# One more zero matmul per unit in twelve stretches of a four-layer attention kernel

## The chip, the core and the metric

The kernel runs on one core of one Trainium2 chip. The metric is device time in microseconds of one execution. Before the change the median of three runs was 1772.71 us, with runs from 1769.92 to 1774.93 us.

## The reference

Two kinds of attention layer alternate, A, B, A, B, over x of shape 1 x 2048 x 512 with 32 heads of width 16. Each layer normalises x, projects it, attends, projects back and adds to x. Cut to what matters:

```
A: four segments of 512 tokens, causal softmax inside each, plus a memory term
   p = softmax(q k^T * 0.25 + mask);  a_dot = p v
   a_mem = phi(q) M / (phi(q) z);  o = g * a_mem + (1 - g) * a_dot
   M += phi(k)^T v;  z += sum phi(k)
B: full attention over all 2048 tokens
   o = softmax(q k^T * 0.25) v
x = x + o @ wo
```

## The kernel before

The kernel is written by a builder in Python. It keeps one list of instructions for each engine, and for each instruction an estimate of when it ends. The estimate (the clock `sc.t` of each engine) decides which piece of work is put into the lists next; the chip then runs each list in its order, with semaphores between engines.

The work is cut into units. A unit is up to three score tiles of 128 keys by up to 512 queries. For each unit TensorE computes the scores into one of two halves of PSUM (banks 0 to 2 and banks 4 to 6, taken in turn). These are matmuls of 32 rows, because a head pair has 32 rows, and different row groups of the array run side by side. ScalarE takes the exponential of a whole unit (L1514) and writes the weights pT to SBUF. In layers of kind A, GpSimd blanks the masked corner of pT (L1529). Two or three units later TensorE multiplies pT with the values (called PV below) and accumulates in bank 7, the accumulation bank. For kind A those matmuls use the whole 128x128 array with few columns of data; for kind B they use 17 of 32 columns of the array with 512 columns of data, four such column groups side by side. In kind B, part of the exponentials is taken from ScalarE and computed on VectorE with integer arithmetic (L1121 and L1184, tiles dxw and others in its place); their scores go to bank 3 or to a bank of the unit.

Between units the builder places background work: projections of the next layer (xT with wA or wB, 128x128, 512 columns), output projections, layer norms, transposes by DMA. All matmuls pass one helper, L445, so that line stands for all of TensorE.

After each unit from the eleventh step on, the loop in `attention` calls `keep_busy`. It looks at the activity of TensorE over the last 3413 ns by the builder's own estimate, and while that lies under 0.5 (0.42 late in the program) it adds a fill: a matmul of a 128x128 block of zeros with 512 columns of wB, accumulated into bank 7, where it adds zero. At most `FILLS` of them are added (1 to 3, set by a table for each part of the program). These are the rows `ps<-wB,zero`.

Of the kernel before, what the change touches and what calls it, by code (L numbers as in the profile page):

```python
# [22 lines left out]
UNIT, DXB, ACC = (0, 4), 3, 7  # L23
# [234 lines left out]
class Builder:  # L258
# [170 lines left out]
    def keep_busy(self):  # L429


        g, n = self.cur, 0
        own = g is not None and g.npv
        if not own and (self.bank_late() > 0 or any(t["next"][0][:1] == ["cont"] for t in self.tasks)):
            return
        bank, al = (self.banks[ACC], g.acc) if own else (self.banks[DXB], self.new_alloc())
        soon = [w.end + LAG[w.eng] for e in self.pvq[:9] if e[0] <= self.unit_no + 1 for w in (self.b_pT[e[4] * 3 + e[5]].last_write,)]
        at = max(self.sc.t["act"] - 1330, min(soon, default=0.0) - self.HOR)
        while n < self.FILLS and self.sc.streamed(max(self.sc.t["pe"], at), 3413) < self.FILL:
            self.mm(self.ps[:, bank.col0:bank.col0 + 512], self.zero[:, :], self.wB[:, 0, 0:512], not own, not own,  # L440
                    [self.b_zero, self.b_wB[0]], bank, al, "fill")
            n += 1

    def mm(self, out, lhsT, rhs, start, stop, reads, bank, alloc, name="", tile=(128, 0, 128, 0), n=512):
        self.sc.add("pe", lambda e: e.matmul(out, lhsT, rhs, start=start, stop=stop, skip_group_check=True),  # L445
                    reads=reads, banks=[(bank, "w", alloc)], name=name, tile=tile + (n,))
# [1312 lines left out]
    def attention(self):  # L1759
        self.flags = {("x", 0, s) for s in range(NSEG)} | {"amem"}  # L1760
        self.xT_free = [0, 1]
        self.dma_at, self.forcing = {}, False
        self.sel, self.pvq, self.deferred, self.qm_free = [], [], [], [0, 1, 2, 3]
        self.qm_late = []

        self.dx_use, self.dx_bufs = [0] * (self.NDX + self.NAREA), list(range(self.NDX))
        self.areas, self.dx_open = self.dx_areas(), set()
        self.dx_build, self.dx_pairs, self.dx_now, self.dxq, self.dx_own = [], [], [None] * self.CHAINS, [], []
        self.dx_seen, self.wide, self.dx_todo = set(), False, 0
        self.wt = set()  # L1770
        self.dx_shut, self.dx_gone = set(), set()
        self.dx_step = self.bank_step = -9
        self.bubble = True
        self.forced, self.low, self.cur, self.gap = 0, True, None, 1
        self.pend = None
        self.nfin, self.oT_owner = {}, {}
        self.cr_pe = self.cr_dve = 0
        self.running, self.filling = None, False
        self.step = self.bg_cols = 0
        self.misc_banks = [DXB]  # L1780
        self.unit_no = 0
        self.parts = {}
        self.pieces = list(self.PIECES)
        self.make_groups()
        self.make_tasks()
        n = 0
        while True:
            items = self.take_banks(2)
            if not items:
                if not self.seqA and not self.seqB and len(self.tasks) == self.CHAINS:  # L1790
                    self.last_out(n)
                    break

                if self.pvq or self.pend:
                    self.step += 1
                    self.pv_step(n + 9, True)
                    self.run_deferred(False)
                    continue
                self.misc_banks = [DXB, 0, 1, 2, 4, 5, 6]
                self.bubble = True  # L1800
                if not self.bg_one():
                    assert self.deferred, ("stuck", [t["next"] for t in self.tasks])
                    self.run_deferred(True)
                continue
            self.misc_banks = [DXB]
            if self.bubble:
                self.bubble, self.cr_pe, self.cr_dve = False, 0, 0
            self.step += 1
            while self.pieces and self.sc.t["act"] >= self.pieces[0][0] * 1000:
                self.__dict__.update(self.pieces.pop(0)[1])  # L1810
            self.near = self.ahead()
            self.dx_widen()
            self.low = self.near < self.LOW
            self.gap = self.GAP if self.near >= self.AHEAD else 1
            isA = items[0][0].kind == "A"
            split = not self.low and not isA
            self.unit_no = n
            self.units = n
            early = self.pend is not None or self.ends(0)
            first = self.pv_step(n) if early else 0  # L1820
            self.compose(n, items)
            self.credit(self.PE_LOW if self.low else self.PE_A if isA else self.PE_B, self.CR_LOW if self.low else self.CR_A if isA else self.CR_W * len(items) / 3 if self.wide else self.CR_B)
            if split and (not self.FIT or not self.wide or self.FIT & 2):
                self.background(True)
            self.cr_dve -= first if early else self.pv_step(n)
            self.run_deferred(False)
            self.background(False if split and not (self.FIT & 1 and self.wide) else None)
            if self.step == 2:
                self.gates()
            left = sum(len(g.banks) - g.pos for g in self.sel)  # L1830
            if not self.seqA and not self.seqB and left <= 3 and not self.parts and len(self.tasks) == self.CHAINS and self.met([("dma", ("oT", 3, 3, c)) for c in range(NCH - 1)]):
                self.last_part(1, self.banks[DXB])
            elif self.step > 10:
                self.keep_busy()
            self.bg_cols = 0
            n += 1

# [48 lines left out]
```

## Time and profile before

| | |
|---|---|
| median of three runs | 1772.71 us (1769.92 to 1774.93) |
| the profiled execution | 1774.13 us |
| its span, first to last instruction | 1772.3 us |
| busy: TensorE, VectorE, ScalarE, GpSimd | 1586.6, 1521.1, 1729.2, 287.2 us |
| mean granted TensorE clock | 0.994 |
| zero matmuls issued | 177 |

Busy time of TensorE counts modelled ends: a matmul of 512 columns is shown as 0.38 to 0.39 us, while the next one can start about 0.21 us after it. The clock of TensorE is shown as the share that was granted in a stretch; 1.00 is full speed.

### The profile page before, as it was taken

What the parts mean: (1) busy time and instruction counts of PE and PEld (TensorE: products, weight loads), DVE (VectorE), ACT (ScalarE), POOL (GpSimd) and SP (SyncE); (2) the same over time, 40 slices, a digit from 0 to 9 for tenths busy, and PEclk for the clock granted to TensorE, in tenths of its full rate; (3) what the DMA queues carried; (4) which work ended last, traced back from release to release, by engine and by line L of the source; (5) the groups of instructions that cost most, each with busy time, mean ns of one, the idle gap of its engine ahead of it and who ended that gap; (6) DMA issues with size and microseconds to landing.
All of it is one profiled execution on the core that took longest, in us unless ns stands there. A gap on an engine that the chain in (4) does not pass through costs nothing.

```text
span 1772.3 us, 42500 instructions
## 1 busy us (share of the span) xinstructions
PE 1586.6 (90%) x17251; PEld 568.1 (32%) x17436; DVE 1521.1 (86%) x3001; ACT 1729.2 (98%) x1674; POOL 287.2 (16%) x656
## 2 busy tenths in 40 slices
PE   7889898889898989989989988988898898889988
PEld 4445454553224222233222332332222222222222
DVE  6677766589995999888999879768999999999997
ACT  7989998999999999999999999999999999999998
POOL 4622515110006000113000240141100000000000
PEclk9999998999999999999999999999999999999999
DMA  6021111000001000000000010110000000000000
GB/s 173 20 46 29 32 20 25 14 9 7 13 7 16 4 13 13 2 19 14 8 13 13 5 34 7 19 26 13 2 13 1 1 7 7 1 1 7 7 1 13
DMA packets 86180, 30.01 MB, mean 17 GB/s; under 512 B 78816, under 2 KB 85472, under 8 KB 85984
## 3 DMA queue, kind: packets, MB, share of 16 engines
q1 hardware_dynamic: 85984, 27.29, 7.6%
q8 instruction: 136, 2.23, 0.5%
q14 instruction: 60, 0.49, 0.1%
HBM read 6.30 MB, written 2.10 MB: 5 GB/s over the span
## 4 chain that ended last, share of the span: by engine, by line
ACT 52%; PE 22%; issue 17%; DVE 6%; POOL 2%; DMA 1%; SPq 0%; ACTq 0%; DVEq 0%; POOLq 0%
ACT pT L1514 51%; PE ps L445 22%; POOL pT L1529 2%; DVE QA L1121 1%; ACT amem L697 0%; DVE dxw L1184 0%; DVE dxw L1121 0%; DMA xT<-xn 0%; DVE rg L809 0%; DVE VB L1121 0%; DVE VB L480 0%; DVE KA L1646 0%; DVE VA L1184 0%; DVE ob L1628 0%; DVE phq L700 0%
## 5 line engine op out<-in xcount | busy, mean ns | idle before, releaser
L1514 ACT ACTIVATE pT<-ps 128x1024 bf16<-128x1024 f32 (+4 forms) x1623 | 1697.0, 1201 | 27.8 <-PE ps L445 21.0
L445 PE MATMUL ps<-qm,KB 32*128 32x512 bf16 x3584 | 517.8, 384 | 79.0 <-ACT pT L1514 67.3
L445 PE MATMUL ps<-pT,VB 128*17 128x512 bf16 x2221 | 377.7, 384 | 8.7 <-ACT pT L1514 3.7
L1529 POOL TENSOR_SCALAR_AFFINE_SELECT pT<-pT 128x256 bf16<-128x256 bf16 (+2 forms) x524 | 213.0, 418 | 548.4 <-ACT pT L1514 535.9
L445 PEld LDWEIGHTS ps<-qm,KB 32*128 32x128 bf16 x3584 | 131.6, 91 | 458.1 <-ACT pT L1514 355.1
L1424 POOL TENSOR_SCALAR qm<-QB,par 128x512 bf16<-128x512 bf16 x88 | 66.9, 763 | 848.7 <-PE ps L445 769.4
L445 PEld LDWEIGHTS ps<-pT,VB 128*17 128x17 bf16 x2221 | 88.1, 87 | 240.0 <-issue 202.5
L1121 DVE TENSOR_SCALAR dxw<-ps 128x512 uint16<-128x512 f32 (+1 forms) x212 | 145.4, 697 | 4.5 <-PE ps L445 3.6
L445 PE MATMUL ps<-qm,KA 32*128 32x384 bf16 (+3 forms) x1024 | 104.3, 307 | 26.0 <-ACT pT L1514 19.5
L1121 DVE TENSOR_SCALAR VA<-ps 128x512 uint16<-128x512 f32 (+1 forms) x172 | 121.4, 720 | 5.8 <-PE ps L445 4.7
L1184 DVE TENSOR_SCALAR dxw<-dxw 128x1024 uint16<-128x1024 uint16 (+1 forms) x302 | 121.0, 411 | 3.5 <-PE ps L445 1.7
L1121 DVE TENSOR_SCALAR QA<-ps 128x512 uint16<-128x512 f32 (+1 forms) x168 | 117.8, 716 | 4.9 <-PE ps L445 4.1
L445 PE MATMUL ps<-qm,QA 32*128 32x512 bf16 x512 | 103.6, 384 | 19.9 <-ACT pT L1514 18.6
L445 PE MATMUL ps<-VA,pT 128*128 128x51 bf16 (+1 forms) x2560 | 108.6, 188 | 14.1 <-POOL pT L1529 6.5
L445 PE MATMUL ps<-dxw,VW 128*17 128x512 bf16 x437 | 108.7, 381 | 0.2 <-DVE dxw L1184 0.2
L445 PEld LDWEIGHTS ps<-VA,pT 128*128 128x128 bf16 x2560 | 85.6, 97 | 63.8 <-POOL pT L1529 30.3
L1121 DVE TENSOR_SCALAR VB<-ps 128x512 uint16<-128x512 f32 (+1 forms) x117 | 92.1, 804 | 2.8 <-PE ps L445 2.1
L1121 DVE TENSOR_SCALAR KB<-ps 128x512 uint16<-128x512 f32 (+1 forms) x98 | 77.9, 808 | 2.5 <-PE ps L445 2.1
L445 PE MATMUL ps<-pT,VA 128*17 128x512 bf16 x386 | 76.7, 384 | 2.2 <-ACT pT L1514 1.8
L445 PE MATMUL ps<-dxw,VB 128*17 128x512 bf16 x256 | 74.1, 381 | 0.0
L445 PE MATMUL ps<-VB,pT 128*128 128x34 bf16 (+1 forms) x1788 | 69.4, 186 | 2.0 <-ACT pT L1514 1.1
L445 PE MATMUL ps<-xT,wB 128*128 128x512 bf16 x224 | 63.0, 393 | 5.8 <-issue 2.7
(292 smaller groups left out, 2408.1 us busy)
## 6 DMA issues: line engine op xcount, KB each, us to landing
out_dram<-x SPq DMA_DIRECT2D x8, 256.0 KB, 2.1
x<-in_A_x_dram SPq DMA_DIRECT2D x3, 512.0 KB, 5.1
wB<-in_B_wqkv_dram SPq DMA_DIRECT2D x1, 1536.0 KB, 11.7
xT<-xn SPq DMA_TRANSPOSE x60, 2.4
oT<-ob SPq DMA_TRANSPOSE x36, 2.4
x<-in_A_x_dram SPq DMA_DIRECT2D x4, 128.0 KB, 2.7
wA<-in_A_wq_dram SPq DMA_DIRECT2D x1, 512.0 KB, 5.1
wA<-in_A_wk_dram SPq DMA_DIRECT2D x1, 512.0 KB, 6.1
```

The source lines that it names most:

```text
L445: self.sc.add("pe", lambda e: e.matmul(out, lhsT, rhs, start=start, stop=stop, skip_group_check=True), reads=reads, banks=[(bank, "w", all ...
L1121: self.sc.add("dve", lambda e: e.tensor_scalar(d, o, SCALE * LOG2E * 128, W_C if dxs[0][:3] in self.wt else EXP_C, op0=ALU.mult, op1=ALU.add),
L1184: self.op("dve", lambda e: e.tensor_scalar(o, w, d, None, op0=ALU.add), reads=self.b_dxw[b0][:len(ents)], writes=wr, ns=(295, 425, 560, 69 ...
L1424: self.op(eng, (lambda m, q, col: lambda e: e.tensor_scalar(m, q, col, 0.0, op0=ALU.mult, op1=ALU.add))(m, q, col), reads=[bq, self.b_par] ...
L1514: self.sc.add("act", (lambda dst, src: lambda e: e.activation(dst, src, ACT.Exp, scale=SCALE))(dst, src), writes=self.b_pT[slot * 3 + i:sl ...
L1529: self.op("pool", (lambda blk, pat: lambda e: e.affine_select(blk, blk, pattern=pat, compare_op=ALU.is_ge, fill=0.0, base=0, channel_multi ...
```

## The change

A new method `quiet` is called after `keep_busy` in every unit. Where the builder's estimate of ScalarE's clock lies in one of twelve fixed stretches, and an accumulation is open in bank 7 that has begun and is not finished, it adds one zero matmul of the same form as a fill. It then puts back the builder's clocks, its list of tiles and its list of activity as they were, so that everything that is decided later is decided as before.

```diff
+    QUIET = ((38, 47), (76, 110), (264, 292), (538, 574), (742, 759), (822, 836), (1018, 1022), (1038, 1052), (1080, 1101), (1168, 1182), (1195, 1202), (1277, 1286))
+
+    def quiet(self):
+
+        sc, g = self.sc, self.cur
+        at = sc.t["act"] / 1000
+        if g is None or not g.npv or g.left == 0 or not any(a <= at < b for a, b in self.QUIET):
+            return
+        held = dict(sc.t), list(sc.tiles), list(sc.streams)
+        bank = self.banks[ACC]
+        self.mm(self.ps[:, bank.col0:bank.col0 + 512], self.zero[:, :], self.wB[:, 0, 0:512], False, False, [self.b_zero, self.b_wB[0]], bank, g.acc, "quiet")
+        sc.ops["pe"][-1].end = held[0]["pe"]
+        sc.t, sc.tiles, sc.streams = held
...
                 self.last_part(1, self.banks[DXB])
             elif self.step > 10:
                 self.keep_busy()
+                self.quiet()
```

In the built lists this adds 139 matmuls to TensorE (316 zero matmuls in place of 177); the lists of the other four engines are the same, and so is TensorE's without the added ones. 90 of the 139 stand in units whose open accumulation is of kind A, 49 in units of kind B. Nineteen, all of kind B, belong to the stretch written 1080 to 1101, 23 to the stretch written 538 to 574 (21 of kind A), 12, all of kind A, to 742 to 759, and five, all of kind A, to 38 to 47. The stretches are in the builder's estimated time; where an added matmul really falls is found by its place in TensorE's list. The helper of all matmuls is L445 before and L459 after.

The first place is TensorE's list in the first A layer, the first of the twelve stretches. The rows `VA,pT` are PV, `qm,KA` are scores of the next unit, `xT,wA` a projection. Before:

```order
L445 MATMUL ps<-VA,pT 128x3x17 x6
L445 MATMUL ps<-qm,KA 128x256 x3
L445 MATMUL ps<-VA,pT 128x3x17 x10
L445 MATMUL ps<-xT,wA 128x512 x4
L445 MATMUL ps<-qm,KA 128x256
L445 MATMUL ps<-qm,KA 128x384 x2
L445 MATMUL ps<-qm,KA 128x128 x2
```

And now:

```order
L459 MATMUL ps<-VA,pT 128x3x17 x6
L459 MATMUL ps<-wB,zero 128x512
L459 MATMUL ps<-qm,KA 128x256 x3
L459 MATMUL ps<-VA,pT 128x3x17 x10
L459 MATMUL ps<-xT,wA 128x512 x4
L459 MATMUL ps<-wB,zero 128x512
L459 MATMUL ps<-qm,KA 128x256
L459 MATMUL ps<-qm,KA 128x384 x2
L459 MATMUL ps<-qm,KA 128x128 x2
```

The added matmul stands at the end of a unit, right ahead of the next unit's scores. In the trace of before the first of these score rows runs at 31.63 us, and the row ahead of which the fifth and last matmul of this stretch is put runs at 37.66 us.

The second place is TensorE's list in the B layer, the ninth stretch, which in the trace of before runs from 1085.5 us. The rows `pT,VB`, `dxw,VW`, `KB,VW` and `VB` are PV in column groups, `qm,KB` are scores. Before:

```order
L445 MATMUL ps<-qm,KB 128x512 x3
L445 MATMUL ps<-pT,VB 17x512 x3
L445 MATMUL ps<-dxw,VW 17x512 x2
L445 MATMUL ps<-KB,VW 17x512 x3
L445 MATMUL ps<-qm,KB 128x512 x3
L445 MATMUL ps<-pT,VB 17x512 x2
L445 MATMUL ps<-KB,VW 17x512
L445 MATMUL ps<-qm,KB 128x512 x3
```

And now:

```order
L459 MATMUL ps<-wB,zero 128x512
L459 MATMUL ps<-qm,KB 128x512 x3
L459 MATMUL ps<-pT,VB 17x512 x3
L459 MATMUL ps<-dxw,VW 17x512 x2
L459 MATMUL ps<-KB,VW 17x512 x3
L459 MATMUL ps<-wB,zero 128x512
L459 MATMUL ps<-qm,KB 128x512 x3
L459 MATMUL ps<-pT,VB 17x512 x2
L459 MATMUL ps<-KB,VW 17x512
L459 MATMUL ps<-wB,zero 128x512
L459 MATMUL ps<-qm,KB 128x512 x3
```

Here a matmul on the whole array now stands between PV in column groups and scores in row groups.

## The prediction

> **What bounds the kernel now.** I read the page first: the span, the busy times and the costliest group.
>
> ```profile
> span 1772.3 us, 42500 instructions
> PE 1586.6 (90%) x17251; PEld 568.1 (32%) x17436; DVE 1521.1 (86%) x3001; ACT 1729.2 (98%) x1674; POOL 287.2 (16%) x656
> L1514 ACT ACTIVATE pT<-ps 128x1024 bf16<-128x1024 f32 (+4 forms) x1623 | 1697.0, 1201 | 27.8 <-PE ps L445 21.0
> ```
>
> ScalarE is the bound: busy 98%, so a microsecond in which it stands still is a microsecond lost. It stands idle ahead of the exponentials for 27.8 us in all, 21.0 of them until TensorE has delivered scores. The change adds nothing to ScalarE, so it can act only through that wait: shorten it where TensorE was slow, lengthen it where TensorE becomes late.
>
> Where was TensorE slow? Next come windows of 3.41 us laid on the edges at which the granted clock changes, and one of the added stretches (columns: length, busy us of PE, PEld, DVE, ACT, POOL with instructions, granted clock, DMA share, GB/s).
>
> ```profile
> 40.61:44.02 3.41, 1.44 (x25) 0.85 (x24) 2.21 (x5) 3.41 (x3) 1.06 (x3) 1.00 0.19 38
> 44.02:47.43 3.41, 3.19 (x23) 1.31 (x23) 0.69 (x1) 2.95 (x5) 1.73 (x4) 0.50 0.00 0
> 88.39:91.81 3.42, 2.03 (x37) 1.10 (x36) 3.35 (x10) 3.27 (x5) 2.73 (x7) 1.00 0.72 82
> 91.81:95.22 3.41, 2.76 (x14) 1.07 (x16) 1.61 (x5) 1.28 (x2) 1.06 (x3) 0.50 0.56 113
> 102.05:105.46 3.41, 1.76 (x14) 0.75 (x15) 2.39 (x6) 2.73 (x4) 2.28 (x5) 1.00 0.77 84
> 105.46:108.87 3.41, 3.27 (x29) 1.73 (x29) 1.67 (x5) 2.15 (x2) 0.00 (x0) 0.50 0.00 1
> 276.13:279.54 3.41, 2.33 (x49) 1.61 (x50) 3.24 (x8) 3.41 (x6) 2.86 (x6) 1.00 0.00 0
> 279.54:289.78 10.24, 9.86 (x98) 5.01 (x99) 4.91 (x14) 7.01 (x10) 5.35 (x15) 0.50 0.41 53
> 1080.00:1101.00 21.00, 18.78 (x167) 5.26 (x170) 20.11 (x44) 21.00 (x22) 0.69 (x1) 1.00 0.01 2
> ```
>
> Four times the clock falls to half, each time after a window in which TensorE was busy 1.44 to 2.33 of 3.41 us. In those half-clock windows ScalarE is not fully busy: 2.95, 1.28, 2.15 and 7.01 us. At 1080 it is busy 21.00 of 21.00: there nothing can be gained and TensorE's lateness can only cost.
>
> **The gain.** The idle times of ScalarE in these places, from its timeline:
>
> ```profile
> 48.47 2.79 ACT L1514 ACTIVATE pT<-ps 128x1536 bf16<-128x1536 f32 x2 [1.50 <-PE ps L445]
> 94.59 1.45 ACT L1514 ACTIVATE pT<-ps 128x1536 bf16<-128x1536 f32 x1 [2.13 <-PE ps L445]
> 105.43 1.45 ACT L1514 ACTIVATE pT<-ps 128x1536 bf16<-128x1536 f32 x1 [0.68 <-PE ps L445]
> 108.14 1.45 ACT L1514 ACTIVATE pT<-ps 128x1536 bf16<-128x1536 f32 x1 [1.26 <-PE ps L445]
> 280.95 2.79 ACT L1514 ACTIVATE pT<-ps 128x1536 bf16<-128x1536 f32 x2 [0.87 <-PE ps L445]
> 284.62 2.07 ACT L1514 ACTIVATE pT<-ps 128x512 bf16<-128x512 f32 x4 [0.88 <-PE ps L445]
> 287.44 1.45 ACT L1514 ACTIVATE pT<-ps 128x1536 bf16<-128x1536 f32 x1 [0.76 <-POOL pT L1529]
> 289.62 3.59 ACT L1514 ACTIVATE pT<-ps 128x1536 bf16<-128x1536 f32 x5 [0.73 <-PE ps L445]
> ```
>
> Together 8.81 us, the upper bound; the lower is nothing, if the falls stay. Which of it goes? TensorE's timeline:
>
> ```profile
> 37.66 0.39 PE L445 MATMUL ps<-qm,KA 32*128 32x256 bf16 x5
> 42.85 0.28 PE L445 MATMUL ps<-qm,KA 32*128 32x256 bf16 x3 [1.97 <-ACT pT L1514]
> 92.46 1.49 PE L445 MATMUL ps<-xT,wB 128*128 128x512 bf16 x3 [1.56 <-DMA xT<-xn]
> 93.88 0.61 PE L445 MATMUL ps<-qm,KA 32*128 32x512 bf16 x3
> 98.79 0.81 PE L445 MATMUL ps<-wB,xT 128*128 128x512 bf16 x3 [0.24 <-ACT pT L1514]
> 105.31 1.78 PE L445 MATMUL ps<-xT,wB 128*128 128x512 bf16 x4
> 109.64 1.04 PE L445 MATMUL ps<-xT,wB 128*128 128x512 bf16 x4
> 1085.84 0.39 PE L445 MATMUL ps<-qm,KB 32*128 32x512 bf16 x3
> ```
>
> The weak window at 40.61 comes from a wait of 1.97 us for ScalarE. The five added matmuls of the first stretch all stand at or ahead of the scores at 37.66, so none falls into it: that fall stays, gain 0. At 92.46 the projection waited for a DMA, and this stays; but three matmuls take 1.49 in place of 0.81 and the scores 0.61 in place of 0.39 us (the last row, at full clock): 0.68 + 0.22 = 0.9 us. At 105.31 four take 1.78 in place of 1.04, 0.74, and the halved scores and PV behind them the rest of 1.26, less a little that remains: 1.1. From 279.5 to 289.8 I count the four idle times, 0.87 + 0.88 + 0.76 + 0.73 = 3.2, since the wait for GpSimd among them is one for a late PV chain behind slow scores. Gain 5.2 us. That one or two matmuls of 0.21 us in a window of 3.41 suffice is not shown by before; it is taken, because windows with busier TensorE do not fall.
>
> The rule: the Trainium skill, page "TensorE: Matmul & The Clock Gate", in its closing table, says that throughput drops mid-kernel are avoided with no idle gap over about 3 us between bursts of matmuls. The trace differs: the longest gap ahead of a fall here is 1.97 us. By the rule no fall would be due and the added matmuls could remove none; the sum would then be that of the rival below in which the falls stay.
>
> **The cost.** What one added matmul takes, in kind A and in kind B:
>
> ```profile
> 753.85 0.38 PE L445 MATMUL ps<-wB,zero 128*128 128x512 bf16 x1
> 757.22 0.59 PE L445 MATMUL ps<-wB,zero 128*128 128x512 bf16 x2
> 757.80 0.28 PE L445 MATMUL ps<-qm,KA 32*128 32x256 bf16 x2
> 759.35 2.02 ACT L1514 ACTIVATE pT<-ps 128x256 bf16<-128x256 f32 x3 [0.34 <-PE ps L445]
> PE ps L445 <- ACT pT L1514: 1.7, 3, 0.8
> PE ps L445 <- ACT pT L1514: 4.3, 9, 1.2
> 1086.16 0.39 PE L445 MATMUL ps<-pT,VB 128*17 128x512 bf16 x2
> 1087.04 0.38 PE L445 MATMUL ps<-KB,VW 128*17 128x512 bf16 x3
> 1087.41 0.39 PE L445 MATMUL ps<-qm,KB 32*128 32x512 bf16 x3
> 1087.74 0.38 PE L445 MATMUL ps<-KB,VW 128*17 128x512 bf16 x1
> 1088.33 0.39 PE L445 MATMUL ps<-qm,KB 32*128 32x512 bf16 x3 [0.20 <-ACT pT L1514]
> PEld ps L445 <- ACT pT L1514: 8.4, 18, 0.8
> ```
>
> Two fills take 0.59, one 0.38: 0.21 us each. In kind A it stands behind matmuls of its own form (or a projection) and ahead of scores, and the change of form there was paid before: 0.21. Over 90 that is 18.9 us. It is hidden where the next scores wait for ScalarE anyway. The two rows of waits of matmuls for ScalarE are those of the stretches 742 to 759 and 538 to 574: 1.7 us against a price of 12 x 0.21 = 2.5, and 4.3 against 21 x 0.21 = 4.4. So between nothing and a third is uncovered even if every wait lay well; the scores at 757.80 follow two fills with no gap, and ScalarE already waits at 759.35. I take a quarter: 4.7 us. Nothing of it at all, and all 18.9, are the bounds.
>
> In kind B scores at 1085.84 are followed by PV at 1086.16: 0.32, that is 0.21 and 0.11 for the change between row groups and column groups. A whole-array matmul between them needs one change more: 0.21 + 0.11 = 0.32 us. Spare time there: PV that began at 1087.04 lets scores begin at 1087.36, they began at 1087.41, spare 0.05; PV of 1087.74 lets them at 1088.06, they began at 1088.33, spare 0.27. Mean 0.16, uncovered 0.16 per unit, the upper end. Lower end: over the stretch from 1080 TensorE's loads wait 8.4 us for ScalarE in 18 waits; an idle of about 0.21 of each is the running out of the PV ahead, leaving 8.4 - 18 x 0.21 = 4.6, against 19 x 0.32 = 6.1, uncovered 1.5 or 0.08 each. ScalarE has no idle there to give. The late scores for VectorE, busy 20.11 of 21.00, lie behind the same matmul, which speaks for the upper end: I take 0.145, and 0.145 x 49 = 7.1 us. All bare would be 49 x 0.32 = 15.7.
>
> No wait is added: the zero block, wB and the accumulation are in place, and the matmul that closes an accumulation stands behind. Cost 4.7 + 7.1 = 11.8 us.
>
> **The sum.** Made against the profiled execution, 1774.13 us (its span 1772.3 and 1.8 around it), 1.4 above the median of the runs and inside their spread: 1774.13 - 5.2 + 11.8 = 1780.7 us.
>
> **The rivals.**
> First, TensorE has room enough. Scores are a unit ahead of ScalarE, so a delay of 0.21 or 0.32 is made up in the next wait; all falls of the stretches go and nothing is paid. 1774.13 - 5.2 = 1768.9, and with all 8.81 us of idle back 1765.3. It decides if ScalarE's idle ahead of exponentials stays what it was in the B stretches. For it speaks the 10% of TensorE not busy; against it the spare of 0.05 at 1087.41.
>
> Second, half the cost is hidden: 1774.13 - 5.2 + 5.9 = 1774.8.
>
> Third, the falls stay or move. The edges of the windows lie on a raster of 3.41 us (91.81 is 14 of them behind 44.02), which need not lie alike in another execution, and other weak places then fall. No gain: 1774.13 + 11.8 = 1785.9. Against it: the weak windows lie in the stretches, but for the first. The Trainium skill says on the same page, in Part 1, that the window runs free and does not restart with the kernel; one trace cannot show it.
>
> Fourth, TensorE becomes the bound in the stretches: all of B and half of A bare, 15.7 + 9.5 = 25.2, so 1774.13 - 5.2 + 25.2 = 1794.1. Against it: 4.3 us of waits in one stretch.
>
> **How the numbers follow.** A difference of 0.3%, 5.3 us, is about what can be told from none: faster is under 1767.4, slower over 1778.0. The forecast, 1775 to 1786 with 1780.7 in it, gets 0.42 (0.32 of it slower, 0.10 same); the first rival 0.25 (0.15 faster, 0.10 same); the second 0.15, same; the third 0.12 and the fourth 0.06, slower. Faster 0.15, same 0.35, slower 0.50. The range reaches into the first rival and over the third: 1766 to 1788.
>
> **What would show it.** Loads of zeros 177 to 316. The clock at 1.00 from 80 to 110 and 264 to 296 us, perhaps half at 44 still. No idle of ScalarE over 0.7 us around 280 to 290. In the B stretches the exponentials, now gapless, show small idle times behind TensorE, some 7 us in all; the waits of TensorE for ScalarE shrink there. If ScalarE's idle behind TensorE falls under 21.0 in total, the cost is wrong; if half clock still stands at 92, 105 or 280, the gain is.

## The result, and the profile after

The changed kernel takes 1779.22 us (median of five runs, 1778.98 to 1781.04) against 1772.71 us before (median of five, 1769.92 to 1774.93): the ratio is 1.0041, with a 95% interval of 1.0027 to 1.0056. It is slower by about 7 us. The profiled execution took 1779.22 us.

The page of the changed kernel, the lines that answer to those of before:

```profile
span 1777.5 us, 42768 instructions
PE 1606.5 (90%) x17380; PEld 574.5 (32%) x17575; DVE 1524.9 (86%) x3001; ACT 1732.8 (97%) x1674; POOL 288.1 (16%) x656
PEclk9999999999999999999999999999999999999999
L1528 ACT ACTIVATE pT<-ps 128x1024 bf16<-128x1024 f32 (+4 forms) x1623 | 1700.5, 1197 | 31.5 <-PE ps L459 23.5
```

Loads of weights for TensorE went from 17436 to 17575, the 139 that were added. The clock shows 9 in every slice, which is 90% or more. Yet ScalarE waits longer for TensorE, 23.5 in place of 21.0 us: it lost more than it won. Of the 5.2 us by which the span grew, ScalarE's idle time is 1.6 us (44.7 in place of 43.1 over the span) and its busy time 3.6 us (1732.8 in place of 1729.2). The busy time is lateness too. In the rows of before that have no gap, an exponential starts before the one ahead of it has ended: at 1079.00, 1079.90 and 1080.89 us, with about 1.02 us each. When scores come late this overlap shrinks, and the page counts that as busy time.

The windows of the changed kernel over the early stretches, over the weak place of the raster that has an added stretch ahead of it, and over the B stretch (columns as in the prediction):

```profile
39.80:43.21 3.41, 2.21 (x28) 1.02 (x27) 2.44 (x6) 3.41 (x4) 1.57 (x5) 1.00 0.19 38
74.00:110.00 36.00, 29.56 (x395) 15.18 (x398) 27.56 (x84) 32.23 (x34) 18.23 (x44) 1.00 0.27 53
264.00:296.00 32.00, 29.14 (x404) 14.92 (x409) 21.27 (x49) 28.75 (x37) 20.50 (x52) 1.00 0.15 30
1080.00:1101.00 21.00, 20.08 (x162) 5.80 (x162) 18.35 (x40) 19.74 (x19) 0.69 (x1) 1.00 0.01 2
```

In these the clock is at 1.00 throughout. In the B stretch ScalarE, busy 21.00 of 21.00 before, is now busy 19.74. Its timeline there, first before, then now, shows gaps that were not there:

```profile
1081.81 26.17 ACT L1514 ACTIVATE pT<-ps 128x1536 bf16<-128x1536 f32 x25
```

```profile
1086.74 1.99 ACT L1528 ACTIVATE pT<-ps 128x1024 bf16<-128x1024 f32 x2 [0.48 <-PE ps L459]
1088.89 1.99 ACT L1528 ACTIVATE pT<-ps 128x1024 bf16<-128x1024 f32 x2 [0.16 <-PE ps L459]
1091.04 1.02 ACT L1528 ACTIVATE pT<-ps 128x1024 bf16<-128x1024 f32 x1 [0.15 <-PE ps L459]
1092.22 1.02 ACT L1528 ACTIVATE pT<-ps 128x1024 bf16<-128x1024 f32 x1 [0.16 <-PE ps L459]
1093.51 7.96 ACT L1528 ACTIVATE pT<-ps 128x1536 bf16<-128x1536 f32 x7 [0.26 <-PE ps L459]
1101.72 4.14 ACT L1528 ACTIVATE pT<-ps 128x1024 bf16<-128x1024 f32 x4 [0.25 <-PE ps L459]
```

And TensorE's timeline shows why:

```profile
1086.57 0.39 PE L459 MATMUL ps<-pT,VB 128*17 128x512 bf16 x2
1086.90 0.39 PE L459 MATMUL ps<-wB,zero 128*128 128x512 bf16 x1
1087.22 0.39 PE L459 MATMUL ps<-qm,KB 32*128 32x512 bf16 x3
1088.08 0.39 PE L459 MATMUL ps<-wB,zero 128*128 128x512 bf16 x1
1088.40 0.39 PE L459 MATMUL ps<-qm,KB 32*128 32x512 bf16 x3
1089.05 0.39 PE L459 MATMUL ps<-wB,zero 128*128 128x512 bf16 x1
1089.37 0.39 PE L459 MATMUL ps<-qm,KB 32*128 32x512 bf16 x3
PEld ps L459 <- ACT pT L1528: 1.4, 3, 0.5
```

From a zero matmul to the scores behind it pass 0.32 us each time. The scores now come every 1.08 us (1087.22 to 1089.37 in two units) where the same ones came 0.92 apart before (1087.41 to 1088.33 in one). The last row, from the waits of the stretch from 1080 to 1101, says that TensorE's loads wait 1.4 us for ScalarE where they waited 8.4: the spare is used up, and now ScalarE waits.

The early gain is to be seen in ScalarE's timeline from 277 us on:

```profile
277.21 8.44 ACT L1528 ACTIVATE pT<-ps 128x1536 bf16<-128x1536 f32 x10 [0.60 <-PE ps L459]
285.97 1.09 ACT L1528 ACTIVATE pT<-ps 128x512 bf16<-128x512 f32 x2 [0.33 <-PE ps L459]
287.99 1.45 ACT L1528 ACTIVATE pT<-ps 128x1536 bf16<-128x1536 f32 x1 [0.93 <-POOL VB L896]
```

Set against each other instruction by instruction, ScalarE of the changed kernel is 6.8 us ahead of before at 340 us (1.1 of it already at 15 us, ahead of any added matmul), stands still at 6.7 up to 536, and is then 5.2 us behind from 1295 us to the end: 12 us lost in the later stretches, 3.4 of them between 1080 and 1108. Of these 3.4 us 2.1 are idle time (ScalarE is busy 25.89 of 28.00 us there, before 28.00); the rest is lost overlap.

### The profile page after: what moved, and what is told of

Same layout as the page of the kernel before. It is cut to its first block, busy times and chain, and to the rows that moved or that the text cites. A ratio compares the mean times of both kernels' runs of the same rounds, so it can differ in the third digit from the quotient of the medians.

```text
span 1777.5 us, 42768 instructions
## 1 busy us (share of the span) xinstructions
PE 1606.5 (90%) x17380; PEld 574.5 (32%) x17575; DVE 1524.9 (86%) x3001; ACT 1732.8 (97%) x1674; POOL 288.1 (16%) x656
## 4 chain that ended last, share of the span: by engine, by line
ACT 49%; PE 25%; issue 16%; DVE 7%; POOL 2%; DMA 0%; SPq 0%; ACTq 0%; DVEq 0%; POOLq 0%
ACT pT L1528 48%; PE ps L459 25%; POOL pT L1543 2%; DVE dxw L1135 1%; DVE QA L1135 1%; DVE dxw L1198 1%; ACT amem L711 0%; DVE VB L1135 0%; DVE ob L1642 0%; DVE KA L1660 0%; DVE VA L1198 0%; DVE x L925 0%; DMA phk<-KA 0%; DVE VA L1135 0%; DVE xT L1135 0%
## 5 line engine op out<-in xcount | busy, mean ns | idle before, releaser
L1528 ACT ACTIVATE pT<-ps 128x1024 bf16<-128x1024 f32 (+4 forms) x1623 | 1700.5, 1197 | 31.5 <-PE ps L459 23.5
L459 PE MATMUL ps<-qm,KB 32*128 32x512 bf16 x3584 | 516.7, 384 | 77.7 <-ACT pT L1528 63.8
L459 PE MATMUL ps<-pT,VB 128*17 128x512 bf16 x2221 | 377.8, 384 | 8.3 <-ACT pT L1528 3.3
L459 PEld LDWEIGHTS ps<-qm,KB 32*128 32x128 bf16 x3584 | 131.2, 91 | 450.8 <-ACT pT L1528 339.9
L459 PEld LDWEIGHTS ps<-pT,VB 128*17 128x17 bf16 x2221 | 88.1, 87 | 240.4 <-issue 203.3
L459 PE MATMUL ps<-VA,pT 128*128 128x51 bf16 (+1 forms) x2560 | 108.8, 187 | 13.7 <-DVE ob L1642 5.9
L459 PE MATMUL ps<-qm,QA 32*128 32x512 bf16 x512 | 103.6, 384 | 17.6 <-ACT pT L1528 16.5
L459 PE MATMUL ps<-qm,KA 32*128 32x384 bf16 (+3 forms) x1024 | 101.9, 302 | 18.6 <-ACT pT L1528 13.1
L459 PE MATMUL ps<-dxw,VW 128*17 128x512 bf16 x437 | 108.9, 381 | 0.3 <-DVE dxw L1198 0.2
L459 PEld LDWEIGHTS ps<-VA,pT 128*128 128x128 bf16 x2560 | 85.4, 96 | 63.2 <-POOL pT L1543 30.0
L459 PE MATMUL ps<-wB,zero 128*128 128x512 bf16 x245 | 81.6, 381 | 2.5 <-issue 1.6
L459 PE MATMUL ps<-pT,VA 128*17 128x512 bf16 x386 | 76.7, 384 | 1.9 <-ACT pT L1528 1.5
L459 PE MATMUL ps<-dxw,VB 128*17 128x512 bf16 x256 | 74.1, 381 | 0.0
L459 PE MATMUL ps<-VB,pT 128*128 128x34 bf16 (+1 forms) x1788 | 69.4, 186 | 2.0 <-ACT pT L1528 1.1
```

Source lines behind the costliest of these rows:

```text
L1528: self.sc.add("act", (lambda dst, src: lambda e: e.activation(dst, src, ACT.Exp, scale=SCALE))(dst, src), writes=self.b_pT[slot * 3 + i:sl ...
```

## The experiments

**The kernel before, unchanged, in more executions.** No edit.

> The kernel before, unchanged, to see how often and where the clock falls in other executions, and what a fall costs. Theory (falls cost ScalarE time, and the spread of before is the spread of falls): the time rises as the mean clock sinks; one half-clock window of 3.41 us is 0.001 of mean clock, and an execution with clock 0.999 is about 4 us faster than one with 0.994; no execution is at 1.000. Rival (the falls of the profiled execution are a chance of that one): most executions stand at 0.999 or 1.000, and their times spread all the same.

The median was 1772.01 us, from 1767.72 to 1776.25 in 12 executions. All 115 executions of before in and beside these experiments (median 1773.24 us) lie close to a line: 1765.4 us at full clock and 1.17 us more for each 0.001 of mean clock that is missing (correlation 0.95; fitted to all 115). The executions beside the experiments were made on four chips; on each of these the mean distance from the line is under 0.3 us. The mean clocks run from 0.989 to 0.998, none is at 1.000; on average 0.0066 is missing. One window of 3.41 us at half clock takes 0.001 from the mean clock over 1772 us, so this is six to seven half-clock windows, 7.7 us. Where they lie changes; this execution fell at 826 and 1045 us as well, where PV of kind A gives way to kind B, and the first one did not:

```profile
82.01:85.43 3.42, 3.42 (x45) 2.37 (x45) 1.32 (x5) 1.94 (x4) 2.17 (x5) 0.50 0.38 77
826.12:832.95 6.83, 6.42 (x57) 2.00 (x60) 5.82 (x13) 5.24 (x5) 0.99 (x2) 0.50 0.23 47
1044.57:1051.40 6.83, 6.66 (x54) 1.80 (x52) 5.52 (x11) 5.28 (x6) 0.42 (x1) 0.50 0.20 41
```

ScalarE is busy only 5.24 and 5.28 of 6.83 us there. The rival is out: no execution stands at 0.999 or 1.000, and the spread of before is nearly all the spread of its falls (the scatter about the line is 0.8 us). This gives a way to split every kernel's time: its mean, less 1.17 us per missing thousandth of clock, less 1765.4, is what its added matmuls cost at full clock. That uses the slope of before for other kernels. It is an assumption, but a line fitted to each kernel's own executions has a slope between 0.99 and 1.26 in seven of the eleven; in the other four (e5_again, e9_spare, e11_spare_late, e12_spare_few) the mean clocks differ by at most 0.003, too little to say.

| kernel | executions | median us | ratio to before, interval | missing clock, thousandths | cost at full clock, us |
|---|---|---|---|---|---|
| e2_early, 38 zeros | 12 | 1772.9 | 0.9994 [0.9983, 1.0005] | 4.3 | 2.8 ± 0.4 |
| e3_B_only, 49 | 8 | 1781.85 | 1.0044 [1.0029, 1.0059] | 7.1 | 8.4 ± 0.7 |
| e4_A_late, 52 | 12 | 1776.51 | 1.0019 [1.0005, 1.0033] | 4.5 | 6.1 ± 0.7 |
| e5_again, 139 | 9 | 1780.38 | 1.0043 [1.0027, 1.0058] | 0.7 | 14.4 ± 0.3 |
| e6_half, 139 of 256 columns | 12 | 1775.42 | 1.0011 [0.9998, 1.0023] | 2.6 | 7.3 ± 0.3 |
| e7_B_short, 49 of 64 columns | 12 | 1775.79 | 1.0019 [1.0004, 1.0033] | 7.5 | 2.3 ± 0.6 |
| e8_B_col, 49 in one column group | 12 | 1774.41 | 1.0011 [0.9997, 1.0025] | 7.1 | 2.1 ± 0.5 |
| e9_spare, 79 | 12 | 1773.67 | 1.0002 [0.9991, 1.0014] | 2.3 | 5.1 ± 0.7 |
| e10_spare_more, 161 | 12 | 1772.62 | 1.0002 [0.9992, 1.0011] | 2.7 | 4.3 ± 0.5 |
| e11_spare_late, 155 | 7 | 1768.67 | 0.9976 [0.9965, 0.9987] | 0.6 | 2.5 ± 0.7 |
| e12_spare_few, 77 | 11 | 1768.9 | 0.9977 [0.9966, 0.9987] | 1.3 | 2.0 ± 0.6 |

The figure behind ± is two standard errors of the executions' scatter about the line, without the line's own error.

**Parts of the change alone.** Three kernels keep only some of the added matmuls:

```diff
+        if at > 300:                            # e2_early
+            return
+        if g.kind == "A":                       # e3_B_only
+            return
+        if at < 300 or g.kind == "B":           # e4_A_late
+            return
```

> Only the 38 added matmuls of the first three stretches (all kind A, up to 300 us of the builder's time), so the gain without the cost of the later stretches. Theory (gain in the early A stretches, cost in the later ones): the clock stays at 1.00 up to 300 us, ScalarE is 5 to 6 us ahead of before there as in the changed kernel and stays ahead to the end: 1767 to 1769 us, ratio 0.997 to 0.998. Rival (the gain is a matter of how the 3.41 us raster lies, so on a mean over executions there is none): 1771 to 1773 us.

> Only the 49 added matmuls in units of kind B. Theory (0.32 us of TensorE each, of which about 0.145 is not covered): 7.1 us over before, 1779 to 1780 us, with the early falls of the clock still there; the ScalarE rows between 1083 and 1106 us show gaps behind TensorE, 3 to 4 us in that stretch. Rival (a unit of lead covers a delay of 0.32 us): 1772 to 1774 us, and no gaps there.

> Only the 52 added matmuls in units of kind A of the stretches from 538 on, where no fall of the clock stood in the profile of before. Theory (a quarter of 0.21 us each is uncovered): 2.7 us over before, at most 5: 1775 to 1777 us. Rival (kind A has room, all of the later cost is kind B): 1772 to 1773 us.

For e2_early the theory was too hopeful: 1772.9 us, where 1767 to 1769 was expected. The first 300 us kept full clock as expected, but falls in the rest of the program stay (4.3 thousandths missing), and 38 matmuls cost 2.8 us. Gain and cost all but cancel. The time is the one that the rival gave, 1771 to 1773 us, but not for the rival's reason: 2.3 thousandths of missing clock are gone. e3_B_only cost 8.4 us at full clock, 0.17 each, and lay over the expected 1779 to 1780; the gaps of ScalarE at 1086 to 1106 are the same as in the changed kernel. These 49 matmuls took no missing clock away: 7.1 thousandths, before 6.6. e4_A_late cost 6.1 us, 0.12 each, over the 5 that the theory allowed; its time lies in the expected 1775 to 1777 us because the clock rose too. The rivals of these two kernels, that nothing is paid, fall. The three costs sum to 17.3 us, the whole costs 14.4; and the three take 3.9 thousandths of missing clock away (e3 adds 0.5), the whole 5.9. Why the parts do not add was not settled.

**The changed kernel again.** No edit beside the change.

> The changed kernel again, beside before on the same chip, in more executions. The executions of before so far lie on a line: 1765.6 us at full clock and 1.13 us more for each 0.001 that is missing of the mean clock. Theory (the added matmuls take the falls away in every execution, 7 us on a mean, and cost about 14 us at full clock): clock 0.999 or 1.000 in nearly all executions, 1778 to 1781 us, with a smaller spread than before. Rival (the five executions with clock 1.000 were a lucky raster): mean clock about 0.996 and 1782 to 1785 us.

Nine executions had clocks of 0.998 to 1.000 and took 1779.13 to 1782.53 us. The gain in clock is no luck of the raster: 0.7 thousandths are missing in place of 6.6.

**Shorter, and in another form.** e6_half has 256 columns in place of 512 in every added matmul; e7_B_short has 64 columns, in kind B alone; e8_B_col, in kind B alone, has 512 columns but 17 columns of zeros in one column group:

```diff
+        self.mm(self.ps[:, bank.col0:bank.col0 + 256], self.zero[:, :], self.wB[:, 0, 0:256], ...)   # e6_half
+        self.mm(self.ps[:, bank.col0:bank.col0 + 64], self.zero[:, :], self.wB[:, 0, 0:64], ...)     # e7_B_short
+        r = min(g.started, key=self.pv_quad)                                                          # e8_B_col
+        self.mm(self.ps[32 * r:32 * r + 17, bank.col0:bank.col0 + 512], self.zero[:, 0:17], self.wB[:, 0, 0:512], ..., tile=(128, 0, 32, 32 * r))
```

> All 139 added matmuls, but with 256 columns of data in place of 512: 0.11 us each in kind A, 0.22 in kind B with the change of form. Theory (the cost is what of the duration TensorE's spare does not cover, so it falls by more than half): 5 to 7 us over 1765.6 at full clock, a mean clock of about 0.997, so 1774 to 1776 us. Rival (the cost is one per instruction, whatever its length): 1778 us or more.

> The 49 matmuls of kind B alone, with 64 columns of data: 0.03 us of data and 0.11 for the change of form. Theory (0.14 us against a spare of 0.16 per unit, so nearly all covered): at most 2 us over 1765.6 at full clock, and with the falls of before 1773 to 1776 us. Rival (the change of form is what is dear, beyond the 0.11 that the rows show): 5 us or more over 1765.6 at full clock.

> The 49 matmuls of kind B alone, with 512 columns of data but 17 zero columns in one column group that has begun, like the PV matmuls around them: no change of form, and beside PV of other groups. Theory (0.21 us at most against a spare of 0.16): 2 to 4 us over 1765.6 at full clock, 1774 to 1777 us with falls. Rival (the stream of 512 columns is the whole price, the change of form nothing): 8 to 9 us over 1765.6 at full clock as for the whole-array form, 1779 us or more.

Half the columns cost 7.3 us, half of 14.4; the upper figure of the theory was 7, so the fall by more than half is not shown, but the rival of a price per instruction is out. In kind B 64 columns with both changes of form cost 2.3 us, a little over the 2 expected. TensorE's timeline of e7_B_short has the short zero matmul between PV and scores:

```profile
1084.95 0.39 PE L461 MATMUL ps<-pT,VB 128*17 128x512 bf16 x2
1085.28 0.20 PE L461 MATMUL ps<-wB,zero 128*128 128x64 bf16 x1
1085.42 0.39 PE L461 MATMUL ps<-qm,KB 32*128 32x512 bf16 x3
```

From zero to scores pass 0.14 us where 512 columns take 0.32, so the time beside the data is 0.11 us. In e8_B_col 512 columns without the changes of form cost 2.1 us; the whole-array form with 512 columns, which has both, cost 8.4. So neither the stream nor the change of form alone is the price: each nearly fits into the spare, their sum does not. The stream is not paid in every unit of e8_B_col, though: in some the zero matmul runs 0.21 us behind PV, in others beside it:

```profile
1088.98 0.38 PE L462 MATMUL ps<-KB,VW 128*17 128x512 bf16 x3
1089.19 0.38 PE L462 MATMUL ps<-wB,zero 128*17 128x512 bf16 x1
1089.51 0.39 PE L462 MATMUL ps<-qm,KB 32*128 32x512 bf16 x3
1089.83 0.39 PE L462 MATMUL ps<-pT,VB 128*17 128x512 bf16 x2
1089.84 0.39 PE L462 MATMUL ps<-wB,zero 128*17 128x512 bf16 x1
1090.15 0.39 PE L462 MATMUL ps<-qm,KB 32*128 32x512 bf16 x3
```

In the second case 0.32 us pass from PV to scores, as without the zero. ScalarE's timeline there is one row without a gap:

```profile
1082.42 24.70 ACT L1531 ACTIVATE pT<-ps 128x1024 bf16<-128x1024 f32 x24
```

But neither form helps the clock: 7.5 and 7.1 thousandths are missing. The whole-array form of 512 columns at the same places does not either (7.1 in e3_B_only), so this is no mark against the forms.

**Zeros only where TensorE stands idle.** If only the uncovered part is paid, zero matmuls in idle places must be nearly free, and weak windows are weak because TensorE is idle there. From the traces of two executions of before I took the places in TensorE's list at which it stood idle, with an accumulation open, for longer than one to three such matmuls take and 0.1 us more, next to weak windows. They are put in by their place in the list, with the builder's state put back as in the change (shortened here; the table is that of e10_spare_more, the other kernels have a shorter one):

```diff
+SPARE = {136: 1, 196: 1, ...}
...
     def mm(self, out, lhsT, rhs, start, stop, reads, bank, alloc, name="", tile=(128, 0, 128, 0), n=512):
+        while name != "quiet" and self.spare.get(at, 0) > 0 and self.cur is not None and self.cur.npv and self.cur.left > 0:
+            self.spare[at] -= 1
...
+            self.mm(self.ps[:, acc.col0:acc.col0 + 512], self.zero[:, :], self.wB[:, 0, 0:512], False, False, [self.b_zero, self.b_wB[0]], acc, self.cur.acc, "quiet")
```

> The kernel before with 79 zero matmuls of the same form, put at 52 places where in the traces of two executions of before TensorE stood idle longer than they take (one to three at a place, with 0.1 us to spare, next to weak windows of the raster), instead of at the end of units. Theory (what is paid is only the part of a zero matmul that TensorE's spare does not cover): 0 to 2 us over 1765.6 at full clock against 14 for the changed kernel, mean clock 0.997 to 0.999 since the places are the idle ones, so 1767 to 1771 us, under before. Rival (every zero matmul costs, wherever it stands, about 0.1 us each): 8 us over 1765.6 at full clock and no gain, 1774 us or more.

> The same with a wider choice of places, 161 zero matmuls at 126 idle places. Theory: 0 to 3 us over 1765.6 at full clock although there are more zeros than in the changed kernel, mean clock 0.998 to 1.000, 1767 to 1771 us. Rival (a price for each): 16 us over 1765.6 at full clock, 1780 us or more.

Both came out level with before, against the theory, and near the rival for 79 (5.1 us, expected 8) but not for 161 (4.3, expected 16). The trace shows another cause. ScalarE lost 4.0 and 5.2 us at 22 to 25 us, and gained, on the whole, from there to the end. The waits of e9_spare's TensorE loads between 14 and 32 us, and ScalarE's timeline:

```profile
PEld ps L458 <- DMA wB<-in_B_wqkv_dram: 2.6, 1, 2.6
24.23 0.60 ACT L491 ACTIVATE KA<-ps 128x512 bf16<-128x512 f32 x1 [3.62 <-PE ps L458]
```

The first zero matmul reads wB, which was still being loaded. Another 0.9 to 1.2 us went at 136 to 139 us. Both places were left out, with the wide and the narrow choice:

> 155 zero matmuls at idle places, without those of the first 30 us (there the zero matmul waited for wB, which was still being loaded, and took 4 to 5 us with it) and without those between 112 and 140 us (1 us lost there). Theory (what lies in spare time is free, and the falls are worth 1.17 us for each 0.001 of clock): 1765 to 1767 us at full clock, mean clock 0.998 to 1.000, 1766 to 1769 us, ratio 0.996 to 0.998, faster than before. Rival (a price for each zero of 0.03 us or more, as the two kernels before seemed to show): 1770 to 1773 us, no gain.

> The same with the narrower choice, 77 zero matmuls at idle places next to weak windows. Theory: as with 155, full-clock time 1765 to 1767 us, mean clock 0.997 to 0.999, 1767 to 1770 us. Rival: half the price of the wider choice and fewer falls removed, 1770 to 1772 us.

Both are faster than before and than the changed kernel: 1768.67 and 1768.9 us, ratios 0.9976 and 0.9977, as the theory expected. What remains is 2.5 and 2.0 us at full clock for 155 and 77 matmuls, 0.016 and 0.026 each, against 0.10 in the changed kernel; the theory allowed 1.6, so they are not quite free. The loss at 22 to 25 us is gone in both traces, which shows its cause. The other is gone in e12_spare_few alone: e11_spare_late still loses 1.0 us around 136, and the changed kernel 0.7, with no added zero there, so its cause is open. Page and timeline of e11_spare_late:

```profile
span 1766.0 us, 42995 instructions
40.07 0.81 PE L458 MATMUL ps<-wB,zero 128*128 128x512 bf16 x3
42.26 0.28 PE L458 MATMUL ps<-qm,KA 32*128 32x256 bf16 x3 [1.38 <-ACT pT L1527]
```

Three zeros now stand in the wait that stood at 42.85 before, and the scores behind them still wait for ScalarE.

## Why the prediction was right

The forecast was 1780.7 us, slower; measured were 1779.22 and, in the second set, 1780.38. Direction and size hold, the size in part by luck, as the sum shows. By its own steps:

- **ScalarE is the bound and the change acts through its wait for TensorE.** Right: 31.5 us of idle in place of 27.8 ahead of exponentials, while 139 matmuls more on TensorE left its own share at 90%. But the idle time behind TensorE rose by only 2.5 us (21.0 to 23.5), where the steps add up to 6.6. The prediction counted lateness as idle time alone; part of it came as lost overlap between exponentials, 3.6 us more of busy time.
- **The gain, 5.2 us.** Right in kind, too small: 5.9 thousandths of clock at 1.17 us are 6.9 us. Two reasons. The fall at 44 was expected to stay, since no added matmul falls into its window; it stands in four of the six profiles without the early matmuls of the change and in none of the four with them; TensorE, made later ahead of it, waits 1.20 us there in place of 1.97 and is busy 2.21 of 3.41 us. That this is the cause was not tried by itself. And one profile did not show that other executions fall at 826 and 1045 too; the third rival had this half: the falls do lie elsewhere in another execution, but the stretches cover most of those places, so they go all the same. What was taken without proof, that windows with busier TensorE do not fall, does not hold beyond the one profile (rows below the list).
- **The price in kind A, 4.7 us, a quarter of 0.21 each.** Too small: 2.8 and 6.1 us when tried in two parts, about 0.10 each, so nearly half was uncovered. The step that was mis-sized is the use of the waits of a whole stretch as if each lay where it was needed. In the two stretches that it was read from, the waits would have left 0.1 us (4.3 against 4.4) and 0.8 us (1.7 against 2.5) uncovered; set against before as above, ScalarE of e4_A_late lost 1.3 us between 536 and 600 and 1.7 between 740 and 780.
- **The price in kind B, 7.1 us, 0.145 each.** 8.4 us, 0.17 each, at the upper end that was worked out from the spare in the timeline (0.16). The half that averaged the stretch's waits pulled it down. That the price on TensorE is 0.21 for data and 0.11 for the change of form is borne out by the rows: 0.32 us from a zero of 512 columns to the scores, 0.14 from one of 64.
- **The sum, 6.6 us.** 7 us, with both terms too small by 1.7 and 2.6 us. That their errors partly cancelled is luck.
- **No idle of ScalarE over 0.7 us around 280 to 290** missed one: 0.93 at 287.99, which is a wait for GpSimd's VB.

Three windows at full clock, two ahead of a fall (e1_before, e12_spare_few) and one of before without a fall behind it:

```profile
822.71:826.12 3.41, 2.65 (x46) 1.49 (x42) 3.33 (x6) 3.41 (x4) 2.28 (x6) 1.00 0.00 0
270.37:273.79 3.42, 2.71 (x53) 1.64 (x54) 3.14 (x9) 3.42 (x5) 2.92 (x6) 1.00 0.00 0
569.70:573.10 3.40, 2.18 (x33) 1.11 (x35) 2.43 (x5) 3.37 (x3) 1.40 (x3) 1.00 0.00 0
```

TensorE is busy 2.65 and 2.71 us ahead of the falls, and 2.18 us where none follows. So the busy time of a window as the profile shows it does not decide alone; what does was not found.

The rule of the Trainium skill, page "TensorE: Matmul & The Clock Gate", closing table, of no gap over about 3 us, would have left no fall to remove and 1785.9 us. The runs decide against it: the falls of before stood behind windows with no gap over 1.97 us, and they went with the added work.

## What to carry to other kernels

Work that keeps an engine's clock up was paid here where that engine had no spare time: read the spare at the very place, unit by unit, from the timeline, because the waits summed over a stretch hide how unevenly it lies. Where such work goes, it should go into the idle places themselves, next to the weak windows: 139 zeros at unit ends cost 14.4 us, 155 and 77 of the same form in idle places 2.5 and 2.0, and the falls went there too (0.6 and 1.3 thousandths missing). Ask of each part what it buys: the 49 zeros of kind B, alone, cost 8.4 us and gained no clock. And a late engine costs more than its idle time shows where its instructions overlap. A time that spreads by 10 us between executions may be a line in another number that each run lists, here the mean clock; fitting it splits gain from cost where a median cannot.

## What the hardware showed that was not expected

The time of before follows the mean clock within 0.8 us (scatter about the line over 115 executions), at 1.17 us per 0.001: about 1.1 us for a half-clock window of 3.41 us, in a kernel whose bound is ScalarE. In the profiles falls inside the program last one, two or three windows of 3.41 us, and no other length. And 49 zero matmuls in units of kind B do nothing for the clock, in one column group or on the whole array (7.1 thousandths missing with either, 6.6 without), while 52 on the whole array in units of kind A bring it to 4.5. Why the place matters so was not tried.
